# Pooling two batches of keys and one of values on GpSimd, the second layer of one more chunk by seven products, and another written-out order

## The chip, the cores and the metric

One NeuronCore of a Trainium2 chip runs the whole computation in one launch. It has five engines, each of which takes its instructions in the order in which they were written: TensorE (PE, with its weight loads as PEld), VectorE (DVE), ScalarE (ACT), GpSimd (POOL) and SyncE (SP, which here only issues transfers). The metric is the device time of one execution in microseconds (us); smaller is better.

## The reference

Attention over pooled keys and values, then a layer norm, a two-layer feed-forward net and a residual:

```
k_p = k.reshape(B, H, 72, 8, 64).mean(axis=3)      # B = H = 8, S = 576, D = 64
v_p = v.reshape(B, H, 72, 8, 64).mean(axis=3)
attn = softmax(q @ k_p^T / 8)                      # over the 72 pooled keys
x = (attn @ v_p), heads side by side               # 8 batches x 576 tokens x 512
xn = (x - mean) / sqrt(var + 1e-6) * g_ln
out = x + relu(xn @ w_ch1) @ w_ch2                 # 512 -> 2048 -> 512
```

All inputs and the output are float32.

## The kernel before

The 4608 tokens are cut into 36 tiles of 128 (t) and nine chunks of four tiles (c = 0 to 8). A tile goes through scores against the pooled keys (`scores`, L748), exponentials and their two float16 halves (`probs`, L776; for the first four tiles `probs_turned`, L803), attention times values, the token's mean and variance and the normalised z (`values`, L865), and z's split into two float16 halves. Every float16 product is made of three matmuls (high by high, high by low, low by high).

Keys and values are pooled once per batch b. `load_k`, `pool_k` (L620 to L630) take a pair of heads at a time: a transfer of 288 KB, one DVE reduction over 8 tokens (L627) and two DVE copies into the block-diagonal `kblk` (L630). `load_v`, `pool_v` (L632 to L640) take a head at a time: a transfer and one DVE reduction (L640). `max_v` and `split_v` (L642 to L720) scale the pooled values and split them, and `spread_v` (L725 to L729) copies them to other partitions by four small transfers, on SP's queue for b = 0 and 1 and on ACT's for later batches. The weights come as raw pairs of integers (`load_raw`, L484), are turned into float32 (`convert`, L489 to L530: DVE maximum L504, two ACT passes, DVE merge L520), get a common scale per half (`max_w1`, `max_w2`) and are split (`split_w` to `split`, L458 to L467).

Layer 1 of chunks 0 and 1 is plain (`ffn_in`, L1058 to L1081, matmul L1070). From chunk 2 on it is Strassen-Winograd's scheme, seven products in place of eight (`product`, L1105 to L1133, matmul L1114), on sums of z (L966 to L973) and of w1 (`sums_w`, L585 to L603). Layer 2 is plain for chunks 0 to 3: `ffn_out` (L1253 to L1276, matmul L1265) makes a tile's half of the sum with 24 matmuls of 512 columns, on the hidden layer that `whole_h` (L1135 to L1144) writes into the ring buffer. From chunk `C_TWO` = 4 on layer 2 is seven products too: `left_factors`, `right_relu`, `right_sums` and `right_pair` (L1154 to L1176, all through `split_h`, L1148 to L1152) make the factors of the hidden layer in the place of w2, and `out_seven` (L1224 to L1251, matmul L1231, sum L1248) makes a product's half with 12 matmuls of 256 columns. The factors of w2 for this are made once by `sums_w2` (L1186 to L1213, in 16 pieces) and `keep_w2`, are kept in DRAM and are brought back by `load_w2`, 512 KB each, 14 per chunk.

The order of all work is written out by hand in two lists of tokens, START (chunks 0 and 1, all preparation of weights, batches 0 to 3 of keys and values) and STEADY (the rest). A token names a step and its arguments; each time that it stands in the list, the step goes on to its next `yield` (`run`, L1360). So A.t is `scores` and `probs` of tile t, B.t `values`, E.t.i `probs_turned`, HK.b.i and HV.b.i half the heads of a batch's keys and values (turn by turn a transfer and its pooling), K0 and V0 batch 0's keys and values, LN, LK, Q, R transfers of tokens, keys, queries and raw weights, C `convert`, M1 and M2 the common scales, S `split_w`, F `ffn_in`, G `ffn_out`, T and U w1's sums, D `spread_v`, P `product`, WH `whole_h`, EL, ER, ES, EP the four factor steps, TW `sums_w2`, KW `keep_w2`, LW `load_w2`, O `out_seven`. Nothing is reordered behind these lists: each engine runs its instructions in list order and waits where an input or a buffer is not ready. START has three PSUM banks for the matmul groups of F and G, STEADY six.

Of the kernel before, what the change touches and what calls it, by code (L numbers as in the profile page):

```python
# [357 lines left out]
def attn_ffn_kernel(ctx: ExitStack, tc: tile.TileContext, qT, kT, v, kvn, kvt, g, w1, w2, out):  # L358
# [265 lines left out]
    def pool_k(b, p):  # L624
# [3 lines left out]
        for j in range(2):  # L628
            r, c = slice(j * D, (j + 1) * D), slice(j * KV, (j + 1) * KV)
            nc.vector.tensor_copy(out=kblk[b % NKB][r, p, c], in_=kp[r])  # L630
# [775 lines left out]
```

## Time and profile before

| | |
|---|---|
| median of 3 runs | 821.44 us (820.87 to 822.48) |
| the profiled execution | 825.36 us, span 823.6 us from the first to the last instruction |
| PE busy | 788.5 us, 96% of the span |
| DVE busy | 655.3 us, 80% |
| ACT busy | 453.5 us, 55% |
| POOL busy | 441.4 us, 54% |
| chain that ended last | PE 75%, DVE 16%, transfers 2%, ACT 2%, POOL 2% |
| mean granted TensorE clock | 0.990 |

A row of a group of instructions gives the line, the engine, the operation, what is written and read, shapes and count; behind the first bar the busy time and the mean duration of one (ns), behind the second the idle time of its engine just before, with what ended it. The view of stretches gives for each stretch of the span the busy time of each engine with its number of instructions, then the granted clock of TensorE, the busy share of the transfer engines and GB/s. Busy time is a union: instructions of one engine overlap at their ends, so means times counts come out somewhat higher.

### The profile page before, as it was taken

The page shows a single profiled execution, that of the slowest core. Times are in us where ns is not written, and L with a number is a line of the kernel's source. Part 1 is how long each engine was busy: PE and PEld are TensorE (multiplying, and loading weights), DVE is VectorE, ACT ScalarE, POOL GpSimd, SP SyncE. Part 2 cuts the span into 40 slices and gives each one's busy share as a digit, 9 for nine tenths or more (in the row PEclk, how much of TensorE's full clock was granted, in tenths as well). Part 3 has the DMA queues.
Part 4 walks back from the last instruction along what each step waited for, and adds up shares of the span by engine and source line. Part 5 has one row for each costly group of instructions (what it writes and reads, how often), then busy time and mean ns, then how long its engine had stood idle before and what let it go on. Part 6 is the DMA issues. An engine that isn't in the chain of part 4 may idle for free.

```text
span 823.6 us, 16934 instructions
## 1 busy us (share of the span) xinstructions
PE 788.5 (96%) x6462; PEld 595.7 (72%) x6462; DVE 655.3 (80%) x1328; ACT 453.5 (55%) x848; POOL 441.4 (54%) x521
## 2 busy tenths in 40 slices
...
GB/s 359 333 125 254 215 126 141 150 90 27 1 106 146 168 157 185 164 158 153 134 105 205 155 190 221 152 243 137 214 146 156 174 178 99 166 166 142 90 104 153
DMA packets 179201, 131.54 MB, mean 160 GB/s; under 512 B 143536, under 2 KB 150832, under 8 KB 176944
## 3 DMA queue, kind: packets, MB, share of 16 engines
...
q10 hardware_dynamic: 1152, 0.90, 0.5%
...
## 4 chain that ended last, share of the span: by engine, by line
PE 75%; DVE 16%; DMA 2%; ACT 2%; POOL 2%; issue 2%; ACTq 1%; DVEq 0%; POOLq 0%
PE ps_f L1114 29%; PE ps_f L1231 19%; PE ps_f L1265 13%; PE ps_f L1070 7%; PE ps_a L754 4%; DVE w L520 2%; DVE w L467 1%; PE ps_a L886 1%; DVE x L1248 1%; PE ps_m L694 1%; PE ps_a L887 1%; DMA vr<-in_v_dram 1%; DVE x L1276 1%; DVE raw L595 1%; DVE wm L504 1%
## 5 line engine op out<-in xcount | busy, mean ns | idle before, releaser
L1114 PE MATMUL ps_f<-zts,w 128*128 128x256 f16 x1680 | 207.2, 273 | 0.9 <-DVE x L1276 0.8
L1231 PE MATMUL ps_f<-ring,w 128*128 128x256 f16 x1680 | 193.7, 273 | 3.8 <-DVE x L1248 2.8
L1231 PEld LDWEIGHTS <-w 128*128 128x128 f16 x1680 | 163.7, 98 | 24.4 <-issue 4.0
L1114 PEld LDWEIGHTS <-w 128*128 128x128 f16 x1680 | 163.4, 98 | 22.1 <-issue 1.5
L1265 PE MATMUL ps_f<-w,ring 128*128 128x512 f16 x768 | 170.0, 379 | 1.5 <-DVE ring L1144 1.4
L1265 PEld LDWEIGHTS <-ring 128*128 128x128 f16 x768 | 74.2, 98 | 88.9 <-DVE ring L1144 3.6
L1133 ACT COPY raw<-ps_f 128x256 f32<-128x256 f32 x168 | 59.1, 372 | 94.3 <-PE ps_f L1114 87.5
L1152 POOL TENSOR_TENSOR w<-w 128x512 f16<-128x512 f32 x64 | 75.1, 1177 | 35.7 <-ACT w L1150 28.4
L1114 PE MATMUL ps_f<-zts,tsp 128*128 128x256 f16 x672 | 91.1, 273 | 0.8 <-ACT raw L1133 0.8
L1070 PE MATMUL ps_f<-zts,w 128*128 128x512 f16 (+1 forms) x480 | 88.4, 343 | 2.5 <-DVE x L1276 1.6
L790 POOL TENSOR_TENSOR phl<-e,phl 128x512 f16<-128x512 f32 x32 | 38.6, 1206 | 73.2 <-ACT phl L780 73.1
L1070 PEld LDWEIGHTS <-w 128*128 128x128 f16 x480 | 47.2, 99 | 40.4 <-issue 6.8
L1150 ACT CAST w<-w 128x512 f16<-128x512 f32 x80 | 48.9, 619 | 46.0 <-POOL w L1170 17.9
L1114 PEld LDWEIGHTS <-tsp 128*128 128x128 f16 x672 | 65.2, 98 | 9.4 <-issue 1.1
L1039 POOL TENSOR_TENSOR hl<-raw,hl 128x640 f16<-128x640 f32 x28 | 40.3, 1444 | 31.6 <-ACT hl L1037 23.2
L1248 DVE SCALAR_TENSOR_TENSOR x<-ps_f,y,x 128x256 f32<-128x256 f32 (+1 forms) x70 | 35.4, 518 | 26.2 <-PE ps_f L1231 25.6
L1248 DVE SCALAR_TENSOR_TENSOR x<-ps_f,cy,x 128x256 f32<-128x256 f32 (+1 forms) x70 | 35.2, 516 | 17.3 <-PE ps_f L1231 16.8
L1128 DVE TENSOR_TENSOR raw<-ps_f,raw 128x256 f32<-128x256 f32 x84 | 34.0, 416 | 18.5 <-PE ps_f L1114 9.6
L754 PE MATMUL ps_a<-kblk,q 128*128 128x144 f32 (+1 forms) x320 | 41.9, 289 | 1.7 <-issue 1.2
L754 PEld LDWEIGHTS ps_a<-kblk,q 128*128 128x128 f32 (+1 forms) x320 | 37.0, 179 | 4.9 <-issue 2.4
L1039 POOL TENSOR_TENSOR hl<-z,hl 128x512 f16<-128x512 f32 x18 | 23.9, 1327 | 30.8 <-ACT hl L1037 16.5
L1079 ACT ACTIVATE ring<-ps_f 128x512 f16<-128x512 f32 (+1 forms) x40 | 19.5, 508 | 37.9 <-PE ps_f L1070 33.3
...
## 6 DMA issues: line engine op xcount, KB each, us to landing
...
```

The lines of the kernel that those rows point to most:

```text
L754: nc.tensor.matmul(ps[r, p // 2, p % 2 * 2 * KV : (p % 2 + 1) * 2 * KV], lhsT=q[:, p, r], rhs=kblk[b % NKB][:, p, :], start=True, stop=True,)
L790: nc.gpsimd.tensor_tensor(out=ph[:, 0, :, KA:P], in0=e[:, :, 0:KA], in1=ph[:, 0, :, 0:KA], op=ALU.subtract)
L1039: nc.gpsimd.tensor_tensor(out=zhl[:, 1, :], in0=src, in1=zhl[:, 0, :], op=ALU.subtract)
L1070: nc.tensor.matmul(ps, lhsT=w[:, part, fs], rhs=zT[:, kz, cols], start=(n == 0), stop=(n == 3 * NKT - 1),)
L1114: nc.tensor.matmul(ps, lhsT=w[:, part, f * P : (f + 1) * P], rhs=z, start=m in (1, 2, 4, 5) and n == 0, stop=m in (2, 3, 4, 7) and n == 3 ...
L1128: nc.vector.tensor_tensor(out=o, in0=ps, in1=o, op=ALU.add)
L1133: nc.scalar.copy(out=o, in_=ps)
L1150: nc.scalar.copy(out=hi, in_=src)
L1152: engine.tensor_tensor(out=lo, in0=src, in1=hi, op=ALU.subtract)
L1231: nc.tensor.matmul(ps, lhsT=wt[2][:, left, part, f * HC + u * P : f * HC + (u + 1) * P], rhs=b[:, f // FPB, wp, f % FPB], start=n < 4 and ...
L1248: nc.vector.scalar_tensor_tensor(out=x, in0=ps, scalar=scale, in1=x, op0=ALU.mult, op1=ALU.add)
L1265: nc.tensor.matmul(ps, lhsT=h[:, part, i, cols], rhs=w[:, wp, j], start=(n == 0), stop=(n == 3 * NFT // 2 - 1),)
```

## The change

Four things change.

1. `pool_k` runs on GpSimd for batches 1 and 2, and `pool_v` for batch 1: three additions of halves (8 to 4, 4 to 2, 2 to 1) take the place of one reduction; for keys the last addition writes `kblk`, once for each of the two heads, so the copies go. The host lays these batches out with the 8 tokens outermost; the bytes of the transfers are the same.
2. `C_TWO` goes from 4 to 3: chunk 3's second layer becomes `out_seven`, with factor steps in place of `whole_h`, and 14 reloads of w2's factors.
3. `LO_GPSIMD` goes from (6, 7, 8) to (): the low halves of `right_pair` with i = 0 in chunks 6, 7 and 8 go from GpSimd to VectorE (24 instructions).
4. Both lists are written anew. In STEADY all 16 TW and 6 KW steps now stand in chunk 2 and at the start of chunk 3. In START, of what the prediction speaks of: the order of the first transfers, A.0 ahead of V0, the places of pooling steps, and B.9 behind HV.2.1.

In `values` the place where a scratch tile is named moves, with the same instructions.

```diff
-C_TWO = 4
+C_TWO = 3
-LO_GPSIMD = (6,7,8)
+K_GPSIMD, V_GPSIMD = (1, 2), (1,)
+LO_GPSIMD = ()
 START = """
-LN.2 LN.2 LK.0 LK.0 LK.1 LK.1 Q.0 Q.0 HK.1.0 R.1.0 R.1.0 V0 V0 K0 K0 K0 HK.1.0 HK.1.0 Q.1 Q.1 R.1.1 R.1.1 R.1.2 R.1.2
-A.0 R.1.3 R.1.3 LG LG A.0 A.0 A.0 E.0.0 V0 V0 E.0.1 A.1 HV.1.0 R.2.0 R.2.0 HK.1.1 A.1 C.1.0 C.1.0 V0 V0 E.0.0 HK.1.0
...
-S.1.2 E.3.1 B.2 E.3.0 E.3.0 S.1.2 S.1.2 S.1.3 C.2.2 C.2.1 E.3.1 E.3.1 B.3 HK.1.1 HK.1.1 R.2.3 R.2.3 A.4 R.1.4 R.1.4 B.1
-B.1 HK.1.1 HK.1.1 A.4 A.5 S.1.3 S.1.3 F.0.0.0 F.0.1.0 F.0.0.0 B.2 F.0.1.0 A.4 A.5 F.0.2.0 A.4 F.0.2.0 C.2.2 HV.1.0
...
-A.8 F.0.7.1 M1.1 B.4 A.6 A.6 A.9 S.2.1 S.2.1 S.2.2 C.1.4 F.0.6.1 S.2.2 S.2.2 S.2.3 F.0.7.1 A.7 C.1.5 C.1.6 F.0.5.1
...
-G.0.1.1 G.0.1.1 HK.3.0 HV.2.1 A.10 HV.2.1 HV.2.1 G.0.3.1 A.11 HV.2.1 HV.2.1 B.8 T.1.0 HV.2.1 HV.2.1 HV.2.1 HV.2.1 A.11
-B.9 F.1.0 F.1.0 T.1.0 HV.3.0 HV.3.0 A.10 A.10 G.0.2.1 A.11 B.9 V.10 F.1.1 F.1.1 HV.3.0 HV.3.0 G.0.2.1 G.0.2.1 A.11 A.11
...
+LK.0 LK.0 Q.0 Q.0 LK.1 LK.1 LN.2 LN.2 R.1.0 R.1.0 HK.1.0 Q.1 Q.1 R.1.1 R.1.1 K0 K0 K0 C.1.0 C.1.0 HK.1.0 HK.1.0 R.1.2
+R.1.2 A.0 R.1.3 R.1.3 A.0 V0 V0 A.0 A.0 E.0.0 E.0.1 E.0.0 E.0.1 A.1 LG LG HV.1.0 HK.1.1 R.2.0 R.2.0 A.1 V0 V0 C.1.1
...
+B.3 B.0 B.0 B.1 A.4 S.1.2 S.1.2 S.1.3 A.4 C.2.2 C.2.1 B.1 B.1 S.1.3 S.1.3 HV.1.0 HV.1.0 B.3 HV.1.1 HV.1.1 B.2 A.4
+HV.1.1 HK.2.0 HK.2.0 D.0 D.0 HV.1.1 A.5 A.4 A.4 A.5 B.2 F.0.0.0 F.0.1.0 F.0.2.0 F.0.0.0 F.0.1.0 C.2.3 F.0.2.0 F.0.0.0
...
+B.4 M1.1 F.0.6.1 C.1.5 F.0.7.1 A.6 A.6 B.4 B.5 C.1.4 C.1.4 C.1.6 C.1.6 S.2.3 S.2.3 G.0.0.0 B.5 B.6 M1.1 M1.1 S.1.4
...
+A.11 F.0.15 B.7 F.0.15 S.2.6 S.2.6 S.2.7 A.10 HV.3.0 HV.3.0 A.10 A.10 B.7 F.0.14 F.0.14 HV.2.1 HV.2.1 HV.2.1 S.2.7
+S.2.7 F.0.15 F.0.15 G.0.0.1 G.0.1.1 G.0.2.1 HV.3.0 HV.3.0 B.6 B.6 HV.3.1 G.0.0.1 G.0.0.1 G.0.0.1 A.11 T.1.0 T.1.0
+HV.3.0 HV.3.0 G.0.1.1 T.1.0 T.1.0 B.8 B.9 G.0.3.1 HV.3.1 HV.3.1 G.0.1.1 G.0.1.1 HV.3.1 G.0.2.1 B.9 V.10 HK.3.0 HK.3.0
...
     def pool_k(b, p):
         kr = kraw.pop((b, p))
-        kp = kr.rearrange("p k l -> p (k l)")[:, 0:KV]
-        nc.vector.tensor_reduce(out=kp, in_=kr, axis=AX.X, op=ALU.add)
+        if b in K_GPSIMD:
+            kr = kr.rearrange("p k l -> p (k l)").rearrange("p (l k) -> p l k", k=KV)
+            nc.gpsimd.tensor_add(out=kr[:, 0:4, :], in0=kr[:, 0:4, :], in1=kr[:, 4:8, :])
+            nc.gpsimd.tensor_add(out=kr[:, 0:2, :], in0=kr[:, 0:2, :], in1=kr[:, 2:4, :])
+        else:
+            kp = kr.rearrange("p k l -> p (k l)")[:, 0:KV]
+            nc.vector.tensor_reduce(out=kp, in_=kr, axis=AX.X, op=ALU.add)
         for j in range(2):
             r, c = slice(j * D, (j + 1) * D), slice(j * KV, (j + 1) * KV)
-            nc.vector.tensor_copy(out=kblk[b % NKB][r, p, c], in_=kp[r])
+            if b in K_GPSIMD:
+                nc.gpsimd.tensor_add(out=kblk[b % NKB][r, p, c], in0=kr[r, 0, :], in1=kr[r, 1, :])
+            else:
+                nc.vector.tensor_copy(out=kblk[b % NKB][r, p, c], in_=kp[r])
...
         vr = vraw.pop((b, h))
-        nc.vector.tensor_reduce(out=vp[b][:, h, :], in_=vr, axis=AX.X, op=ALU.add)
+        if b not in V_GPSIMD:
+            nc.vector.tensor_reduce(out=vp[b][:, h, :], in_=vr, axis=AX.X, op=ALU.add)
+            return
+        vr = vr.rearrange("p d l -> p (d l)").rearrange("p (l d) -> p l d", d=D)
+        nc.gpsimd.tensor_add(out=vr[:, 0:4, :], in0=vr[:, 0:4, :], in1=vr[:, 4:8, :])
+        nc.gpsimd.tensor_add(out=vr[:, 0:2, :], in0=vr[:, 0:2, :], in1=vr[:, 2:4, :])
+        nc.gpsimd.tensor_add(out=vp[b][:, h, :], in0=vr[:, 0, :], in1=vr[:, 1, :])
```

601 lines of the change are left out of this document (311 added, 290 removed).

## The prediction, written before the result was known

> **What bounds the kernel now.** I read the stretches of the span first, then TensorE's waits, then the chain of waits, then VectorE's timeline. Stretches (us: length; busy time and instructions of PE, PEld, DVE, ACT, POOL; granted clock, transfers):
>
> ```profile
> 0.00:50.30 50.30, 38.27 (x314) 29.18 (x314) 40.77 (x76) 32.66 (x42) 17.29 (x25) 0.93 0.81 304
> 50.30:85.00 34.70, 29.51 (x272) 25.02 (x270) 30.83 (x68) 30.41 (x50) 14.13 (x15) 1.00 0.74 195
> 85.00:150.00 65.00, 64.96 (x367) 32.19 (x366) 62.31 (x123) 42.71 (x57) 27.67 (x25) 1.00 0.65 172
> 150.00:165.00 15.00, 12.42 (x71) 5.77 (x70) 9.23 (x20) 2.52 (x4) 3.33 (x5) 0.77 0.63 121
> ...
> 245.00:340.00 95.00, 92.78 (x760) 66.85 (x759) 78.36 (x179) 48.20 (x97) 40.01 (x59) 1.00 0.64 155
> 340.00:440.00 100.00, 98.75 (x737) 67.47 (x736) 83.65 (x177) 50.10 (x104) 52.14 (x73) 1.00 0.65 157
> ...
> 600.00:824.00 224.00, 215.78 (x2046) 192.23 (x2044) 149.94 (x298) 125.41 (x259) 153.75 (x173) 0.99 0.50 140
> ```
> From 245 us, where START's last matmul ends, PE is busy nearly all the time: 2.2 us are free in 245 to 340, 1.3 in 340 to 440. There only fewer matmuls can help. START is different. Up to 50.3 us PE lacks 12.0 us, up to 85 another 5.2, and in 150 to 165 another 2.6 at a granted clock of 0.77 (a loss of (1 - 0.77) x 15 = 3.5 us). DVE is busy 30.8 of 34.7 us before 85 and 62.3 of 65 after it. So START is set by what VectorE must do before PE can go on.
>
> ```profile
> PE ps_m L694 <- DMA w<-in_kvn_dram: 6.2, 1, 6.2
> ...
> PE ps_a L886 <- DMA va<-vh: 2.6, 1, 2.6
> ```
> ```profile
> 6.21 7.32 PE ps_m L694 x10
> ...
> 50.40 2.73 PE ps_f L1070 x24
> ...
> 150.90 4.50 DMA va<-vh
> ...
> 224.33 20.73 PE ps_f L1265 x96
> ...
> 799.63 18.36 PE ps_f L1231 x168
> ```
> The waits name the first and the late hole: the first matmul waits 6.2 us for tokens, and attention times values waits 2.6 us for `va`, the spread values of batch 2, a transfer of 4.50 us. VectorE's timeline shows the middle:
>
> ```profile
> 8.10 1.35 DVE L1336 TENSOR_REDUCE w<-w 128x144 f32<-128x1152 f32 x1 [5.31 <-DMA w<-in_kT_dram]
> ...
> 15.53 0.68 DVE L644 TENSOR_REDUCE mv<-vp 72x1 f32<-72x512 f32 x1
> ...
> 49.90 1.28 DVE L467 SCALAR_TENSOR_TENSOR w<-w,gs 128x1024 f16<-128x1024 f32 x1
> ```
> At 8.10 us batch 0's keys are there, at 15.53 V0's maximum begins, and at 49.90 + 1.28 = 51.2 us the last split of w1's first half ends, which the first layer-1 matmuls (50.40) need. Between 15.53 and 51.2 DVE is idle for hardly a moment.
>
> **The change, part by part.** The sum is made against the profiled execution (825.36 us, span 823.6), which is 3.9 us above the median of 821.44; I take the differences and subtract them from the median.
>
> *Chunk 3's second layer.* Plain: 2 halves x 4 tiles x 24 = 192 matmuls at 20.73 / 96 = 216 ns, 41.5 us. Seven products: 2 x 7 x 2 x 12 = 336 at 18.36 / 168 = 109 ns, 36.7 us. On the path, since PE is full there: -4.7 us. What comes with it:
>
> ```profile
> L1248 DVE SCALAR_TENSOR_TENSOR x<-ps_f,y,x 128x256 f32<-128x256 f32 x60 | 28.2, 480 | 21.1 <-PE ps_f L1231 20.7
> ...
> L1144 DVE SCALAR_TENSOR_TENSOR ring<-raw,ring 128x512 f16<-128x512 f32 x32 | 23.6, 781 | 2.1 <-ACT ring L1140 2.0
> ...
> L1169 POOL TENSOR_TENSOR w<-raw 128x256 f32<-128x256 f32 x26 | 21.2, 814 | 34.0 <-ACT raw L1161 32.6 <-DVE w L1152 0.9
> ...
> L1276 DVE SCALAR_TENSOR_TENSOR x<-ps_f,cy,x 128x512 f32<-128x512 f32 x28 | 20.7, 742 | 2.6 <-PE ps_f L1265 2.1
> ...
> L1152 DVE TENSOR_TENSOR w<-raw,w 128x512 f16<-128x512 f32 x26 | 19.2, 746 | 2.5 <-ACT w L1150 2.5
> L1206 POOL TENSOR_TENSOR phl<-kr,phl 128x512 f16<-128x512 f32 x16 | 18.8, 1180 | 12.4 <-ACT phl L1204 7.9 <-DMA w2s<-phl 4.6
> ...
> L1152 DVE TENSOR_TENSOR w<-raw,w 128x256 f16<-128x256 f32 x26 | 15.3, 588 | 2.4 <-ACT w L1150 2.4
> L1193 DVE TENSOR_TENSOR kr<-w 128x256 f32<-128x256 f16 x32 | 13.9, 475 | 2.1 <-POOL phl L1206 2.0
> ...
> L1152 DVE TENSOR_TENSOR w<-w 128x512 f16<-128x512 f32 x16 | 13.7, 858 | 0.3 <-ACT w L1150 0.3
> ...
> L1199 POOL TENSOR_TENSOR kr<-kr 128x128 f32<-128x128 f32 x16 | 7.6, 478 | 1.3
> ```
> DVE loses 8 x 0.742 (sums) and 16 x 0.781 (`whole_h`) = 18.4 us and gets 24 sums of 0.480, 4 double ones at about 0.742, and 8 x (0.746 + 0.588 + 0.858) of splits = 32.0 us: +13.6. The eight DVE pairs of w2's second half (16 x 0.475 = 7.6) go from chunk 3 to chunk 2. So DVE comes to 78.4 + 7.6 = 86 of 95 us in chunk 2 and 83.7 - 7.6 + 13.6 = 90 of about 95 in chunk 3: hidden, with little room. POOL's piece of `sums_w2` is four additions near 0.478 and one of 1.18, 3.1 us; eight of them, 24.7 us, move to chunk 2 (40.0 becomes 65 of 95), and chunk 3 gets 8 x (4 x 0.814 + 1.18) = 35.5 (52.1 becomes 63). ACT is half idle in 340 to 440. 14 reloads of 512 KB are 7.3 MB in 95 us, some 77 GB/s on 157, below the 304 that the first stretch carries. Queued behind the new POOL and DVE steps are PSUM sums (L1248, L1128) and with them PE's banks. I take +2 us of new waits for all this, between 0 and 5 (half of DVE's 10 us of room gone).
>
> *`LO_GPSIMD`.* 24 subtractions leave POOL (24 x 1.18) and cost DVE 24 x 0.858 = 20.6 us in 600 to 824, where it is busy for 149.9 of 224 us: nothing; without that room, 20.6.
>
> *Pooling.* Rows of what goes, of narrow GpSimd additions, and of two DVE steps that are moved:
>
> ```profile
> L640 DVE TENSOR_REDUCE vp<-vr 72x64 f32<-72x512 f32 x56 | 37.1, 673 | 3.2 <-DMA vr<-in_v_dram 3.1
> ...
> L764 DVE TENSOR_REDUCE mx<-ps_a 128x8 f32<-128x576 f32 x36 | 27.0, 751 | 13.5 <-PE ps_a L754 13.2
> ...
> L769 DVE TENSOR_TENSOR e<-ps_a,mx 128x576 f32<-128x576 f32 x32 | 24.2, 758 | 2.4
> ...
> L630 DVE COPY kblk<-kr 64x72 f32<-64x72 f32 x56 | 20.9, 373 | 1.3
> L627 DVE TENSOR_REDUCE kr<-kr 128x72 f32<-128x576 f32 x28 | 20.8, 742 | 0.1
> ...
> L793 POOL TENSOR_TENSOR phl<-e,phl 128x64 f16<-128x64 f32 x32 | 13.7, 428 | 0.0
> ```
> Off DVE: 8 pairs x (0.742 + 2 x 0.373) + 8 heads x 0.673 = 17.3 us. Onto POOL: the trace has no such addition, but its neighbours. Keys: 288 wide between 0.814 (256) and 1.18 (512), nearest 0.88; 144 wide 0.52 (0.478 at 128); two of 72 at 0.43 each: 2.3 us a pair. Values: 0.81 + 0.48 + 0.43 = 1.7 us a head. In all 32 us, in a queue that was busy for 31.4 of the first 85 us. Batch 1 alone makes 23 of it and comes before 85: 54. Ahead of the first tiles' low halves of z (L858), which the first layer-1 matmuls need, stand batch 1's four pairs and three heads, 14 us more than the at most 17 so far: from the first landing, which I estimate near 12.5 us by the rate below, that ends by 44 plus waits, below 50. So hidden, but not by much.
>
> *START's order, up to the first layer-1 matmul.* The keys (two transfers of 576 KB) and Q.0 (256 KB) now go ahead of the tokens (1152 KB). Before, tokens had landed at 6.21 and the first 576 KB of keys at 8.10: 303 KB/us after 2.4 us of start. So all keys are there at about 7, K0 ends at 8.9, and V0's matmuls, 7.3 us, run from 10.9 to 18.2 instead of 6.2 to 13.5. V0's maximum moves from 15.5 to about 18.8, and DVE, in order, waits for it. From there to the last split it had 35.7 us. It sheds three pairs (3 x 1.49), one head (0.67) and one maximum of w1 (1.21, done while it waits), and gets A.4's scores (0.751 + 0.758) and a merge (1.22): -3.6. The last split ends at 18.8 + 32.1 = 50.9: no gain (between -2 and +2), but A.4 is done.
>
> *From there to layer 2 of chunk 0 (85.0).*
>
> ```profile
> 73.34 0.68 DVE L640 TENSOR_REDUCE vp<-vr 72x64 f32<-72x512 f32 x1 [2.50 <-DMA vr<-in_v_dram]
> ...
> 83.52 0.15 DVE L425 TENSOR_SCALAR rowmax<-rowmax 128x1 int32<-128x1 int32 x1
> ...
> 84.99 5.35 PE L1265 MATMUL ps_f<-w,ring 128*128 128x512 f16 x24
> ```
> DVE reached the end of M1.1's row maxima at 83.7 us, 32.5 after the split. A.4 and the merge are done (-2.7), seven heads are gone (-4.7), the wait of 2.50 for values' transfers falls on POOL, and two small steps come ahead (at most a merge's 1.2): 23.8, so about 75. Then PE is the bound: it was busy for 29.5 of the 34.7 us, has one score step less and one small step more (29.0, an estimate half a us lower): so 79.4. ACT, 30.4 busy less A.4's three steps, has nearly as much to do: +1. Layer 2 (L1265) at 80.4 instead of 85.0: -4.6 us, between 0 (nothing) and -6.
>
> *The spread of batch 2.* Before, its transfer is issued directly ahead of B.9 in PE's order; now G.0.0.1, G.0.1.1 and G.0.2.1 (3 x 24 x 216 ns = 15.5 us) lie between. That covers 4.50 us. The hole of 2.6 us and the low clock behind it (3.5) go: up to -6.1; at worst 0, if VectorE comes to the split later. I take -5.
>
> *Two engines on one port.* The pooled batches went through DVE's reductions; the additions read two operands.
>
> ```profile
> L520 DVE SCALAR_TENSOR_TENSOR w<-w,tsp x8: 1211/1217/1231, 21.9 to 116.3; 128x1024 int32<-128x1024 int32 x8
> ...
> L520 DVE SCALAR_TENSOR_TENSOR w<-w,ring x2: 1216/1698/2180, 37.5 to 38.7; 128x1024 int32<-128x1024 int32 x2
> ...
> L858 POOL TENSOR_TENSOR zts<-z,zts x4: 1152/1160/2226, 37.5 to 63.0; 128x512 f16<-128x512 f32 x4
> ```
> DVE's merge takes 1.22 us, once 2.18; POOL's subtraction 1.15, once 2.23, at the same moment (37.5): both lose 1 us. POOL gets 23 us more in the first 85 us, from 37% busy to 64%; of DVE's some 16 wide merges and splits there about 4 more are hit, and the POOL ones with them. I take +2.5, from 0 to 6. The Trainium skill (SBUF — State Buffer, section "Who interferes with whom") says that a DVE instruction with two SBUF inputs contends for a whole instruction with a GpSimd one that reads SBUF, and a reduction never does. That speaks against this move; the two long rows agree, and by it alone every one of the 16 could be hit, a sum 13 us worse.
>
> Sum: -4.7 + 2 - 4.6 - 5 + 2.5 = -9.8 us: **811.6** (span near 814).
>
> **Rivals.**
> 1. *Only the products count.* The late V0 takes what the lighter DVE gives, PE reaches layer 2 at 85 as before, and another spread waits instead (D.1 stands 4 us ahead of B.4). For it: ACT is as full as DVE before 85. Against: DVE's list is shorter by 17.3 us. 821.4 - 4.7 + 1 = 817.7.
> 2. *START gains all and nothing is lost.* -6 - 6.1 - 4.7: 804.6. For it: PE was full for 65 us beside a DVE busy for 62.3 of them. Against: the port rows.
> 3. *The products bring nothing:* chunk 3's factors and reloads come late by the 4.7 us, START stays: 821.4. For it: these factors pass through DVE and POOL before PE has them, and both get fuller in this stretch. Against: with DVE at 83.7 of 100 PE lost 1.3 us.
> 4. *Slower: GpSimd late in front of chunk 3.* All 16 pieces of w2's sums must be in DRAM and read out before chunk 3's first factor may overwrite w2. 16 x 3.1 + the other 15.3 us of that stretch = 65 us of POOL in PE's 95. This decides once port conflicts stretch POOL by more than 95 / 65 = 1.47; the worst row stretches by 2226 / 1152 = 1.93, the median not at all. At 1.6 it is 104, 9 late, and 3.5 at low clock: 811.6 + 12.5 = 824.1. The Trainium skill (TensorE: Matmul & The Clock Gate, Part 1) has the clock at half until about 3.4 us of work have gone by, a loss of half of that; in 150 to 165 the loss is twice as large, 3.5 us, and the row decides.
>
> **How the numbers follow.** Forecast 0.36, rival 1 0.26, rival 2 0.15, rival 3 0.10, rival 4 0.13. A median of this kernel is known to some 0.2% (1.6 us; its three runs spread by that). Faster: forecast, rivals 1 and 2, a little of 3: 0.78. Same: most of 3, 0.08. Slower: rival 4 and a part of the open waits, 0.14. The bounds of the forecast's terms reach from rival 2's 804.6 to 827; leaving out 2 in 10, 804 to 823.5.
>
> **What would show it.** Right: L1231 x2016 and L1265 x576; PE's matmuls of the first layer near 50 us and of layer 2 near 80; no wait for `va` with a clock under 1 near 150; PE free for about 2 us per 100 in chunks 2 and 3; L627 x20, L640 x48, and 56 new POOL additions. Wrong: V0's maximum later than 20 us or the first layer-1 matmul after 53; merges (L520) often near 2 us; PE waiting in chunk 3 for factors, sums or `ring`; VectorE full and PSUM sums late in chunks 2 to 5.

## The result and the profile after

The changed kernel takes 831.25 us (median of 4 runs, 830.86 to 831.60) beside 821.15 us for the kernel before on the same chip. The ratio is 1.0118, with a 95% interval of 1.0102 to 1.0135: slower by 1.2%, where 1.2% faster had been forecast. The profiled execution has a span of 829.9 us (before: 823.6). Its stretches, in the columns explained above:

```profile
0.00:50.30 50.30, 38.57 (x312) 29.61 (x312) 35.90 (x64) 30.22 (x39) 29.78 (x47) 0.97 0.77 286
50.30:85.00 34.70, 29.42 (x271) 25.35 (x271) 30.92 (x59) 33.53 (x52) 29.77 (x42) 1.00 0.77 242
85.00:150.00 65.00, 62.15 (x340) 30.53 (x341) 62.59 (x112) 42.56 (x57) 34.29 (x32) 0.95 0.72 175
150.00:165.00 15.00, 15.00 (x110) 7.54 (x108) 14.33 (x32) 4.27 (x8) 6.46 (x9) 1.00 0.84 206
...
243.00:300.00 57.00, 55.23 (x462) 40.71 (x462) 49.13 (x109) 28.75 (x60) 31.85 (x49) 1.00 0.75 185
300.00:340.00 40.00, 33.74 (x230) 21.41 (x229) 35.94 (x75) 18.98 (x37) 29.62 (x41) 0.96 0.55 126
...
480.00:520.00 40.00, 32.66 (x286) 27.78 (x286) 31.79 (x60) 18.78 (x36) 17.66 (x24) 0.96 0.52 139
```

The same two late stretches of the kernel before:

```profile
300.00:340.00 40.00, 38.63 (x284) 25.49 (x283) 33.49 (x79) 21.64 (x43) 21.68 (x31) 1.00 0.64 156
...
480.00:520.00 40.00, 39.64 (x382) 35.62 (x380) 32.12 (x67) 22.92 (x45) 21.09 (x25) 1.00 0.94 225
```

Two things are to be seen. Up to 85 us GpSimd is busy for 59.6 us in place of 31.4, and PE is no better off. And PE, which lacked 1.4 and 0.4 us in the two late stretches, now lacks 6.3 in 300 to 340 and 7.3 in 480 to 520, each at a granted clock of 0.96. TensorE's waits (us in total, times, longest) name who is late; some 29 of the 38 us are put down to VectorE:

```profile
PE ps_a L785 <- DVE kblk L1370: 7.3, 2, 6.6
PE ps_f L1262 <- DVE w L1183: 4.6, 5, 3.3
PE ps_a L917 <- DVE x L935: 3.8, 1, 3.8
PE ps_f L1262 <- DVE x L1279: 3.8, 3, 2.2
PE ps_f L1145 <- DVE raw L1159: 3.0, 2, 2.1
...
PE ps_f L1296 <- DVE x L1307: 2.8, 1, 2.8
```

(Lines have moved: L754 is now L785, L1070 L1101, L1114 L1145, L1152 L1183, L1231 L1262, L1248 L1279, L1265 L1296, L1276 L1307.) The wait for `va` of before is gone. The first row is no new loss: 6.6 us of it are the first matmul's wait for batch 0's keys, in the place of the 6.2 us for tokens of before.

What VectorE did around the hole at 490 to 501 (three waits of PE, 6.3 us together) stands in its timeline (start, length, line, operation):

```profile
492.06 1.11 DVE L1032 TENSOR_TENSOR a<-y 128x4 f32<-128x4 f32 x1
493.20 0.23 DVE L1033 TENSOR_TENSOR a<-a,ve 128x4 f32<-128x4 f32 x1
493.47 1.32 DVE L1034 SCALAR_TENSOR_TENSOR y<-a,y 128x4 f32<-128x4 f32 x1
494.71 0.47 DVE L1279 SCALAR_TENSOR_TENSOR x<-ps_f,y,x 128x256 f32<-128x256 f32 x1
495.10 0.79 DVE L1032 TENSOR_TENSOR a<-y 128x4 f32<-128x4 f32 x1
495.93 1.32 DVE L1033 TENSOR_TENSOR a<-a,ve 128x4 f32<-128x4 f32 x1
497.29 0.65 DVE L1034 SCALAR_TENSOR_TENSOR y<-a,y 128x4 f32<-128x4 f32 x1
...
499.45 1.05 DVE L1034 SCALAR_TENSOR_TENSOR y<-a,y 128x4 f32<-128x4 f32 x1
```

The split of L1183 that PE waits for (3.3 us) comes right behind, at 500.42. These are the refinement steps of chunk 5's token scales (`token_scales`): nine operations on 128 x 4 numbers, seven of them shown. In the views of their lines the median length is 0.16 us; here the nine come to 6.8. GpSimd's timeline beside them:

```profile
491.81 1.34 POOL L821 TENSOR_TENSOR phl<-e,phl 128x512 f16<-128x512 f32 x1
...
493.38 1.39 POOL L1070 TENSOR_TENSOR hl<-raw,hl 128x640 f16<-128x640 f32 x1
494.73 1.15 POOL L1183 TENSOR_TENSOR w<-w 128x512 f16<-128x512 f32 x1
495.84 1.40 POOL L1070 TENSOR_TENSOR hl<-raw,hl 128x640 f16<-128x640 f32 x1
497.20 0.72 POOL L1203 TENSOR_TENSOR w<-raw,w 128x256 f32<-128x256 f32 x1
...
499.33 1.15 POOL L1183 TENSOR_TENSOR w<-w 128x512 f16<-128x512 f32 x1 [0.73 <-ACT w L1181]
```

Each long small operation ends within 0.04 us of the end of a GpSimd instruction: 493.17 and 493.15, 494.79 and 494.77, 495.89 and 495.88, 497.25 and 497.24, 497.94 and 497.92, 500.50 and 500.48. The sum of L1279 in the middle, which reads PSUM, takes its ordinary 0.47. So a first theory: a small VectorE operation waits for a whole GpSimd instruction, and whatever stands behind it in VectorE's queue, and PE, waits too.

In START the same picture stands ahead of PE's wait of 3.8 us (VectorE, then PE, then GpSimd):

```profile
82.33 2.77 DVE L924 COPY cvm<-cv 64x3 f32<-64x3 f32 x2
...
85.70 0.69 DVE L935 TENSOR_TENSOR x<-ps_a,rs 128x512 f32<-128x512 f32 x1
```
```profile
86.54 0.21 PE L917 MATMUL ps_a<-va,pt 128*128 128x65 f16 x1 [3.84 <-DVE x L935]
...
87.39 3.17 PE L1296 MATMUL ps_f<-w,ring 128*128 128x512 f16 x7
```
```profile
82.19 2.13 POOL L481 TENSOR_TENSOR w<-w 128x1024 f16<-128x1024 f32 x1 [2.63 <-ACT w L479]
```

Two copies of 64 x 3 numbers take 2.77 us beside a GpSimd subtraction of 2.13.

### The profile page after: what moved, and what is told of

Read it like the earlier page. It is cut to its first block, busy times and chain, and to the rows that moved or that the text cites. A ratio compares the mean times of both kernels' runs of the same rounds, so it can differ in the third digit from the quotient of the medians.

```text
span 829.9 us, 17329 instructions
## 1 busy us (share of the span) xinstructions
PE 787.7 (95%) x6606; PEld 612.1 (74%) x6606; DVE 661.5 (80%) x1348; ACT 468.8 (56%) x880; POOL 482.5 (58%) x593
## 4 chain that ended last, share of the span: by engine, by line
PE 74%; DVE 18%; POOL 4%; ACT 2%; issue 1%; DMA 1%; SPq 0%; DVEq 0%; POOLq 0%
PE ps_f L1145 26%; PE ps_f L1262 23%; PE ps_f L1296 11%; PE ps_f L1101 7%; PE ps_a L785 3%; DVE w L1183 2%; DVE w L537 2%; DVE x L1279 1%; PE ps_a L917 1%; PE ps_a L918 1%; DVE mx L795 1%; PE ps_m L725 1%; DVE w L484 1%; DVE x L1307 1%; DVE kr L1224 1%
## 5 line engine op out<-in xcount | busy, mean ns | idle before, releaser
L1262 PE MATMUL ps_f<-ring,w 128*128 128x256 f16 x2016 | 235.2, 274 | 8.9 <-DVE w L1183 4.6
L1262 PEld LDWEIGHTS <-w 128*128 128x128 f16 x2016 | 196.9, 98 | 35.9 <-DVE w L1183 6.3
L1145 PE MATMUL ps_f<-zts,w 128*128 128x256 f16 x1680 | 207.8, 273 | 1.0 <-DVE x L1307 0.8
L1145 PEld LDWEIGHTS <-w 128*128 128x128 f16 x1680 | 163.4, 98 | 21.6 <-issue 1.8
L1296 PE MATMUL ps_f<-w,ring 128*128 128x512 f16 x576 | 128.9, 384 | 2.9 <-DVE x L1307 2.8
L1296 PEld LDWEIGHTS <-ring 128*128 128x128 f16 x576 | 56.6, 99 | 70.7 <-issue 6.3
L1145 PE MATMUL ps_f<-zts,tsp 128*128 128x256 f16 x672 | 92.7, 276 | 6.2 <-DVE raw L1159 3.0
L1101 PE MATMUL ps_f<-zts,w 128*128 128x512 f16 (+1 forms) x480 | 85.7, 336 | 2.9 <-POOL zts L889 1.5
L1181 ACT CAST w<-w 128x512 f16<-128x512 f32 x96 | 58.7, 619 | 51.8 <-POOL w L1204 27.1
L1145 PEld LDWEIGHTS <-tsp 128*128 128x128 f16 x672 | 66.0, 99 | 15.9 <-issue 7.3
L1183 POOL TENSOR_TENSOR w<-w 128x512 f16<-128x512 f32 x48 | 58.0, 1208 | 32.9 <-ACT w L1181 21.2
L1101 PEld LDWEIGHTS <-w 128*128 128x128 f16 x480 | 46.5, 98 | 38.4 <-issue 4.2
L1279 DVE SCALAR_TENSOR_TENSOR x<-ps_f,y,x 128x256 f32<-128x256 f32 (+1 forms) x84 | 42.7, 517 | 33.5 <-PE ps_f L1262 32.9
L1200 POOL TENSOR_TENSOR w<-raw 128x256 f32<-128x256 f32 x32 | 25.7, 802 | 62.4 <-ACT raw L1192 33.0
L1279 DVE SCALAR_TENSOR_TENSOR x<-ps_f,cy,x 128x256 f32<-128x256 f32 (+1 forms) x84 | 42.1, 516 | 15.4 <-PE ps_f L1262 14.8
L785 PE MATMUL ps_a<-kblk,q 128*128 128x144 f32 (+1 forms) x320 | 43.7, 294 | 9.5 <-DVE kblk L1370 7.3
L1070 POOL TENSOR_TENSOR hl<-raw,hl 128x640 f16<-128x640 f32 x28 | 40.6, 1453 | 13.1 <-ACT hl L1068 13.1
L785 PEld LDWEIGHTS ps_a<-kblk,q 128*128 128x128 f32 (+1 forms) x320 | 38.2, 183 | 12.4 <-DVE kblk L1370 7.7
L1183 DVE TENSOR_TENSOR w<-raw,w 128x512 f16<-128x512 f32 (+1 forms) x64 | 42.6, 667 | 2.5 <-ACT w L1181 2.4
L1159 DVE TENSOR_TENSOR raw<-ps_f,raw 128x256 f32<-128x256 f32 x80 | 32.2, 417 | 13.9 <-PE ps_f L1145 8.0
```

What stands on the lines that cost most here:

```text
L785: nc.tensor.matmul(ps[r, p // 2, p % 2 * 2 * KV : (p % 2 + 1) * 2 * KV], lhsT=q[:, p, r], rhs=kblk[b % NKB][:, p, :], start=True, stop=True,)
L1070: nc.gpsimd.tensor_tensor(out=zhl[:, 1, :], in0=src, in1=zhl[:, 0, :], op=ALU.subtract)
L1101: nc.tensor.matmul(ps, lhsT=w[:, part, fs], rhs=zT[:, kz, cols], start=(n == 0), stop=(n == 3 * NKT - 1),)
L1145: nc.tensor.matmul(ps, lhsT=w[:, part, f * P : (f + 1) * P], rhs=z, start=m in (1, 2, 4, 5) and n == 0, stop=m in (2, 3, 4, 7) and n == 3 ...
L1159: nc.vector.tensor_tensor(out=o, in0=ps, in1=o, op=ALU.add)
L1181: nc.scalar.copy(out=hi, in_=src)
```

## The experiments

All ratios are to the kernel before, run beside each kernel, with 95% intervals. Its own median was 822.6 to 823.3 us in these series, so differences between kernels are taken between their ratios, times 822.5 us, and not between their times. The rival theory throughout is that VectorE simply has too much to do in these places, in any order and whatever GpSimd does.

### Where the loss lies: START, STEADY, pooling

*e1*: the changed kernel with the old STEADY list.

```diff
-C_TWO = 3
+C_TWO = 4
-LO_GPSIMD = ()
+LO_GPSIMD = (6, 7, 8)
-STEADY = (new list)
+STEADY = (list of the kernel before)
```

> The changed kernel with the old STEADY list (chunk 3's second layer plain, low halves of chunks 6 to 8 on GpSimd): of the change, only START's order and the pooling on GpSimd are left. Theory (START is worth the 2 us by which its last matmul came earlier, 243.0 instead of 245.1, and the loss is all in STEADY): 819 us, 817 to 821. Rival A (START hands over something late, a key, a value or a sum, that STEADY pays for): 824 or more. Rival B (START's gain was real but eaten behind it by the new STEADY only): 814 or less.

Measured: 822.8 us, ratio 1.0006 (0.9992 to 1.0021). START's order and the pooling together are worth nothing; the theory's 2 us, read off one matmul, were not there.

*e2*: the other half, with the old START and the pooling on VectorE.

```diff
-K_GPSIMD, V_GPSIMD = (1, 2), (1,)
+K_GPSIMD, V_GPSIMD = (), ()
-START = (new list)
+START = (list of the kernel before)
```

> The old START list with the old pooling on VectorE, and the new STEADY list (chunk 3 by seven products, all low halves of right_pair on VectorE). Theory (the loss is STEADY's): the 2 us of START come back on top of 831.3, so 833 us, 830 to 836, with the holes near 305, 330 and 490 us still there, 2 us later. Rival A (the loss comes from START or from pooling on GpSimd): 817, the old time less the 4.7 us of the products.

Measured: 831.3 us, 1.0102 (1.0069 to 1.0135). All of the loss is STEADY's, and it doesn't need the pooling or the new START.

*e3*: both new lists, pooling back on VectorE (the first two lines of e2's diff).

> The changed kernel with both lists as they are, and all pooling back on VectorE (K_GPSIMD and V_GPSIMD empty). If GpSimd is the engine that the front of START waits for (theory: it stands in the chain of waits from 30 to 65 us), the first layer-1 matmul comes earlier than 53.1 us, but VectorE, 93 of 100 us busy from 50 to 150, gets 17 us more and layer 2 of chunk 0 comes later than 87.4: 834 us, 831 to 838. Rival (what the pooling on GpSimd costs in conflicts is as much as it saves): 829 to 831, START's last matmul within 1 us of 243.

Measured: 839.6 us, 1.0202 (1.0174 to 1.0230), 6.9 us slower than the change. The direction was expected, one part of the reason was not: the first layer-1 matmul comes at 59.7 us, not before 53.1, and layer 2 of chunk 0 at 98.2. With this order VectorE can't carry the pooling.

### The hole at 490 us

*e4*: the nine operations with one input each.

```diff
-nc.vector.tensor_tensor(out=a, in0=y, in1=y, op=ALU.mult)
-nc.vector.tensor_tensor(out=a, in0=a, in1=ve, op=ALU.mult)
-nc.vector.scalar_tensor_tensor(out=y, in0=a, scalar=1.5, in1=y, op0=ALU.subtract, op1=ALU.mult)
+nc.vector.tensor_scalar(out=a, in0=y, scalar1=1.0, scalar2=0.0, op0=ALU.mult, op1=ALU.add)
+nc.vector.tensor_scalar(out=a, in0=a, scalar1=1.0, scalar2=0.0, op0=ALU.mult, op1=ALU.add)
+nc.vector.tensor_scalar(out=y, in0=a, scalar1=-1.0, scalar2=0.0, op0=ALU.mult, op1=ALU.add)
```

> The changed kernel, with each of the three operations of the three refinement steps of the token scales (128 x 4 elements, on VectorE) replaced by one that reads one tensor in place of two: the same number, size, place and engine. Left out is the refinement itself, so the scales are rough. Theory (at 492 to 500 us these nine each wait for a whole GpSimd instruction because both read two tensors; 1.46 us of work takes 6.9, and the splits behind them on VectorE, and so TensorE's factors, come late by that): the nine fall back to 0.16 us each, the hole of 6.3 us there goes with the low clock behind it, and the time is 824 us, 822 to 826. Rival (VectorE simply has too much to do there and the order is wrong): 831, 830 to 832, with the hole in its place.

Measured: 833.3 us, 1.0122 (1.0091 to 1.0153): no gain. Taken alone this speaks for the rival. VectorE's timeline says otherwise:

```profile
493.55 1.12 DVE L1032 TENSOR_SCALAR a<-y 128x4 f32<-128x4 f32 x1
494.70 0.23 DVE L1033 TENSOR_SCALAR a<-a 128x4 f32<-128x4 f32 x1
494.96 1.32 DVE L1034 TENSOR_SCALAR y<-a 128x4 f32<-128x4 f32 x1
```

The one-input operations last as long as the two-input ones, to 0.01 us; the three shown here end within 0.03 us of a GpSimd instruction. The experiment had not removed the wait, so it could not tell the theories apart; what fell is "because both read two tensors". The Trainium skill (SBUF — State Buffer, section "Who interferes with whom") has this: beside operations with two inputs in SBUF it lists copies and TENSOR_SCALAR as able to contend with GpSimd, in the modes in which they use two ports for one tensor, and says of reductions that they never do on this chip. The rows of e4 agree with the first half (no row shows the mode), those of e5 with the second.

*e5*: the same nine as reductions over an axis of length 1.

```diff
-(the three operations)
+nc.vector.tensor_reduce(out=a, in_=y.unsqueeze(2), axis=AX.X, op=ALU.add)
+nc.vector.tensor_reduce(out=a, in_=y.unsqueeze(2), axis=AX.X, op=ALU.add)
+nc.vector.tensor_reduce(out=y, in_=a.unsqueeze(2), axis=AX.X, op=ALU.add)
```

> As e4_one_input, but each of the nine operations is a reduction over an axis of length 1 (TENSOR_REDUCE, 128 x 4 out of 128 x 4 x 1). In e4 the one-input TENSOR_SCALAR had waited just as long as the two-input ones (1.12, 0.23, 1.32 us for 1.11, 0.23, 1.32), so it didn't tell contention from order. The rows of the changed kernel beside GpSimd's work show reductions at their ordinary time (0.67 us for values at 501.0). Left out are the refinement and the sign of the scales. Theory (these nine wait for GpSimd's instructions, and the rest of VectorE's queue and TensorE behind it): about 0.16 us each at 492 to 500, the hole of 6.3 us gone, 824 us, 822 to 826. Rival (VectorE's list is too long there whatever the operations): 831, 830 to 833.

Measured: 824.8 us, 1.0024 (1.0010 to 1.0038), 7.7 us less than the change, as the theory had it (7.3). (The reduction at 501.0 us that the expectation points to had no GpSimd instruction beside it, so it showed nothing yet.) Same place, number and size; only the form differs:

```profile
492.44 0.14 DVE L1032 TENSOR_REDUCE a<-y 128x4 f32<-128x4 f32 x1
492.62 0.16 DVE L1033 TENSOR_REDUCE a<-y 128x4 f32<-128x4 f32 x1
492.81 0.16 DVE L1034 TENSOR_REDUCE y<-a 128x4 f32<-128x4 f32 x1
492.88 0.47 DVE L1277 SCALAR_TENSOR_TENSOR x<-ps_f,y,x 128x256 f32<-128x256 f32 x1
```

0.16 us each where they had been up to 1.32. From 480 to 520 us PE is busy for 36.5 us in place of 32.7, at a clock of 1.00 in place of 0.96, which is some 5.5 us of the 7.7; the rest lies elsewhere, since the steps of all chunks were changed. This settles the cause of most of that hole: not the amount of VectorE's work, and not the order by itself, but small operations that wait for GpSimd, in front of work that PE needs.

*e6*: the order instead of the form.

```diff
-... TS.5 O.4.1.1.1 O.4.1.1.1 TS.5 HV.6.1 ... A.24 TS.5 EP.4.1.3.0 ... HK.6.0 HK.6.0 O.4.1.6.0 ...
+... O.4.1.1.1 O.4.1.1.1 HV.6.1 ... A.24 EP.4.1.3.0 ... HK.6.0 HK.6.0 TS.5 TS.5 TS.5 O.4.1.6.0 ...
```

> The changed kernel with one edit of order: the three refinement steps of chunk 5's token scales (tokens TS.5, nine operations of 128 x 4), whose result is first needed near 550 us, stand some 50 tokens later, behind HK.6.0, where GpSimd has a pause. Same work, same forms. Theory (they stood in front of the splits and sums that TensorE waits for while GpSimd ran six instructions in a row): the hole at 490 to 501 shrinks from 6.3 us to 1 or less and takes the low clock behind it with it (1.8 us): 824 us, 822 to 826. Rival (VectorE is full there and the next operation is late instead): 829 or more.

Measured: 827.2 us, 1.0043 (1.0028 to 1.0059), 6.2 us less than the change: near the theory's 7.3, far from the rival. All nine take 0.16 to 0.17 us there. Between 480 and 507 us PE still loses 3.8 us in six waits of 0.2 to 0.9 us; four of them had been there, two (one for GpSimd, one for VectorE) are new.

*e7*: the refinement on GpSimd, with four operations a step.

```diff
-nc.vector.tensor_tensor(...), nc.vector.tensor_tensor(...), nc.vector.scalar_tensor_tensor(...)
+nc.gpsimd.tensor_tensor(out=a, in0=y, in1=y, op=ALU.mult)
+nc.gpsimd.tensor_tensor(out=a, in0=a, in1=ve, op=ALU.mult)
+nc.gpsimd.tensor_scalar(out=a, in0=a, scalar1=1.5, scalar2=1.0, op0=ALU.subtract, op1=ALU.mult)
+nc.gpsimd.tensor_tensor(out=y, in0=a, in1=y, op=ALU.mult)
```

> The changed kernel with the refinement of all token scales on GpSimd in place of VectorE (four operations a step, as the fused one isn't used there; some 0.15 to 0.25 us each). Theory: at 492 to 500 VectorE is free of the wait, 824 us, 822 to 827; GpSimd's queue gets 12 small operations a chunk, 2 to 3 us, with room. Rival (GpSimd is what is late at this place, its sums feed the splits): 831 or more.

Measured: 828.1 us, 1.0059 (1.0040 to 1.0079), 4.9 us less than the change: the theory holds, with less to gain than by moving.

*e8*: e6, and chunk 3's token scales later too.

```diff
-... TS.3 TW.1.2.0 TS.3 TS.3 TS.3 G.2.0.1 ... P.3.0.2.6 P.3.0.2.6 ...
+... TW.1.2.0 G.2.0.1 ... P.3.0.2.6 TS.3 TS.3 TS.3 TS.3 P.3.0.2.6 ...
```

> As e6_ts5_later, and the last steps of chunk 3's token scales (TS.3, at 326 to 330 us in front of a sum for which TensorE waits 2.8 us) stand 130 tokens later too; their result is first needed near 360. Theory: 2.2 us of stretched small operations leave that place, the wait of 2.8 falls to 1 or less: 821.5 us, 819.5 to 824. Rival: as e6, 824, because the sum there is late for other reasons.

Measured: 825.0 us, 1.0026 (1.0015 to 1.0037). PE's wait of 2.8 us for L1307 is gone; a new one of 1.6 us ends at 357 (at 352 in e12, where START is shorter), ahead of which the moved operations now lie (nine; the expectation of e14 counts them as eleven). Against e6 it is 1.4 us less (expected 2.5). Moving 7 tokens of 3398 has brought 7.6 us of STEADY's loss back.

### START

*e9*: the change with one line edited.

```diff
-nc.vector.tensor_copy(out=cv[r], in_=CV[b][r])
+nc.vector.tensor_reduce(out=cv[r], in_=CV[b][r].unsqueeze(2), axis=AX.X, op=ALU.add)
```

> The changed kernel with the two copies of 64 x 3 elements that tiles over a batch's border need (line 924, eight instructions in the whole span) written as reductions over an axis of length 1: the same values. In START they took 2.77 us at 82.3 us beside a GpSimd instruction of 2.13, ordinarily 0.3, and TensorE waited 3.84 us there for what follows them. Theory (START's expected gain goes into such waits behind GpSimd): that hole shrinks by 2.4 us, layer 2 of chunk 0 begins near 85 instead of 87.4, and since TensorE is full from there to 243 all of it and some of the clock's loss stays: 828.5 us, 827 to 829.5. Rival (the splits of w1 and the sums of values in the same queue are late anyway): 831.

Measured: 828.0 us, 1.0061 (1.0040 to 1.0082), 4.7 us less than the change, somewhat more than expected (2.8). VectorE and PE at that place:

```profile
82.27 0.30 DVE L924 TENSOR_REDUCE cvm<-cv 64x3 f32<-64x3 f32 x2
```
```profile
84.01 0.19 PE L917 MATMUL ps_a<-va,pt 128*128 128x65 f16 x1 [1.38 <-DVE x L935]
```

2.77 us became 0.30, PE's wait of 3.84 became 1.38, and layer 2 of chunk 0 begins at 84.5 in place of 87.4.

*e10* is e8 with e9's line, *e11* is e1 with e9's line, *e17* is the kernel before with it.

> e8_ts3_ts5_later and the copies of e9_cvm_reduce together. Theory: the two add, 825.0 less 2.4 to 3.5: 822 us, 820.5 to 823.5. Rival (what comes earlier in START is lost again in STEADY, where VectorE is full): 824.5 or more.

> The new START with pooling on GpSimd, the old STEADY (chunk 3 plain), and the copies of line 924 as reductions. Theory: 822.8 less 2.4 to 3.5, so 820 us, 818.5 to 821, less than the kernel before. Rival: 822.8, as without the edit.

> The kernel before with one edit: the copies of line 893 (64 x 3, tiles over a batch's border) as reductions. Of the eight, one took 1.5 us there and none stands in front of a wait of TensorE. Theory (the 4 us of e11 are START's new order, freed of its worst wait): no change, 823, 822 to 824. Rival (the edit is worth as much in any kernel): 820 or less.

Measured: e10 821.2 us, 0.9976 (0.9961 to 0.9991), 4.1 less than e8; e11 **818.8 us, 0.9952 (0.9937 to 0.9968)**, 4.4 less than e1 and faster than both kernels; e17 823.0 us, 0.9989 (0.9969 to 1.0009), no change. All three go the theory's way: the line is worth its wait where it stands ahead of PE, and nothing elsewhere.

*e13*: e11 with two of the three additions of each pooling left out.

```diff
-nc.gpsimd.tensor_add(out=kr[:, 0:4, :], in0=kr[:, 0:4, :], in1=kr[:, 4:8, :])
-nc.gpsimd.tensor_add(out=kr[:, 0:2, :], in0=kr[:, 0:2, :], in1=kr[:, 2:4, :])
-nc.gpsimd.tensor_add(out=vr[:, 0:4, :], in0=vr[:, 0:4, :], in1=vr[:, 4:8, :])
-nc.gpsimd.tensor_add(out=vr[:, 0:2, :], in0=vr[:, 0:2, :], in1=vr[:, 2:4, :])
```

> e11_e1_cvm (new START, old STEADY, copies as reductions; 818.8 us) with only the last of the three halvings of each pooled key pair and value head on GpSimd: left out are the first two, so 6 of 8 tokens, and 8 x 1.29 + 8 x 1.2 = 20 us of GpSimd's work up to 107 us. Theory (what START was expected to gain and did not is taken by GpSimd's additions and the waits of VectorE behind them): first layer-1 matmul near 51 in place of 53, START's end 2 to 4 us earlier: 815.5 us, 814 to 817. Rival (the order has no more to give; the first transfers and VectorE's own list set it): 818 to 819.

Measured: 814.3 us, 0.9891 (0.9867 to 0.9916), 5.0 us less than e11. The first layer-1 and layer-2 matmuls of e13, then those of e11:

```profile
50.58 0.60 PE L1081 MATMUL ps_f<-zts,w 128*128 128x256 f16 x4
...
80.36 0.81 PE L1276 MATMUL ps_f<-w,ring 128*128 128x512 f16 x3
```
```profile
53.31 0.93 PE L1085 MATMUL ps_f<-zts,w 128*128 128x256 f16 x7
...
84.81 1.04 PE L1280 MATMUL ps_f<-w,ring 128*128 128x512 f16 x3
```

The forecast had 50.9 and 80.4. With most of GpSimd's additions gone both places are reached when they were forecast, and the additions are what the order is short of: 2.7 us at layer 1, 4.5 at layer 2, 5.2 at START's end (235.5 in place of 240.7). How much of that is GpSimd's own queue and how much VectorE's waits behind it, this run can't tell: it takes both away. In the chain of waits of the changed kernel GpSimd is the path from 51.2 to 71.7 us, and the pooling's additions are 11.1 us of that.

### What is left in STEADY

*e12* is e10 with batch 4's keys on GpSimd too, *e14* is e12 with TS.3's steps at a third place, *e16* is e14 with the keys of batches 5 to 7 on GpSimd as well.

```diff
 e12: -K_GPSIMD = (1, 2)      +K_GPSIMD = (1, 2, 4)
 e14: -... P.3.0.2.6 TS.3 TS.3 TS.3 TS.3 ...   +... P.3.0.3.3 P.3.0.3.3 TS.3 TS.3 TS.3 TS.3 EL.3.0.3 ...
 e16: -K_GPSIMD = (1, 2, 4)   +K_GPSIMD = (1, 2, 4, 5, 6, 7)
```

> e10_e8_cvm with the keys of batch 4 pooled on GpSimd too: four reductions and eight copies (4 x 1.12 us) leave VectorE at 282 to 299 us, where they stand in front of the sums and hidden halves for which TensorE waits 4.2 us at 302 to 307, and GpSimd, which waits 5.96 and 5.99 us for VectorE there, gets 4 x 2.1. Theory A (in chunk 2 VectorE has too much to do, not only waits behind GpSimd): 2 to 4 us less than e10. Theory B (what counts there is the waits behind GpSimd, and these get more): no change or 1 to 3 us more.

> e12_keys4_gp (820.2 us) with TS.3's last steps at a third place, behind P.3.0.3.3 near 357 us, where both VectorE and GpSimd pause. At the second place (344 to 347 us) eleven small operations take 2.7 us in front of a score step, and TensorE waits 1.62 us at 352. Theory: that wait goes, nothing new comes: 818.5 us, 817.5 to 819.5. Rival (VectorE is full there in any order): 820 or more.

> e14_ts3_third (819.5 us) with the keys of batches 5, 6 and 7 on GpSimd too: 12 reductions and 24 copies, 13.4 us, leave VectorE between 360 and 600 us, GpSimd gets 12 x 2.1 = 25 us there. Theory A (VectorE has too much to do in chunks 3 to 5): as for batch 4, 0.3 us a pair, 816 to 818. Theory B (what is left are waits of VectorE behind GpSimd): 819.5 to 822.

Measured: e12 820.2 us, 0.9959 (0.9945 to 0.9972); e14 819.5 us, 0.9957 (0.9937 to 0.9976); e16 823.0 us, 0.9998 (0.9981 to 1.0015). The steps from e10 to e12 and from e12 to e14 are each within what the intervals leave open (e12 was between its two theories); the wait of 1.6 us at 352 is gone in e14, its small operations take 0.15 to 0.23. e16 is 3.4 us slower than e14, as the theory of waits has it: VectorE's busy time falls by 7.1 us, where the expectation had 13.4 us of work leave it, and PE waits more often.

*e15* is e12 and *e18* is e11, each with the other setting of `LO_GPSIMD`.

```diff
 e15: -LO_GPSIMD = ()          +LO_GPSIMD = (6, 7, 8)
 e18: -LO_GPSIMD = (6, 7, 8)   +LO_GPSIMD = ()
```

> e12_keys4_gp with the low halves of right_pair of chunks 6 to 8 back on GpSimd, as before the change (24 subtractions). Forecast on record for this part: nothing, hidden in VectorE's room from 600 us on: 820, 819 to 821.5. Rival (fewer wide instructions on GpSimd are fewer waits for VectorE, and the change gained by it): 822 or more. Rival (VectorE was nearer to its limit there): 818.5 or less.

> e11_e1_cvm (818.8 us: new START, pooling on GpSimd, old STEADY, copies of line 924 as reductions) with the low halves of right_pair of chunks 6 to 8 on VectorE, as in the change. Theory (24 wide subtractions fewer on GpSimd are fewer waits of VectorE, worth the 1.2 us that e15 lost): 817.6 us, 816.5 to 818.5. Rival (hidden in VectorE's room, as forecast): 818.8.

Measured: e15 821.4 us, 0.9982 (0.9967 to 0.9996), 1.9 more than e12, with intervals that overlap; e18 822.1 us, 0.9987 (0.9969 to 1.0005), 2.9 more than e11, with intervals that just don't. So the 24 subtractions on VectorE do no harm with the new list and cost 2.9 us with the old one; why, no run shows. The expectation for e18, which carried e15's number to another list, was wrong.

## Why the prediction was wrong

START's end is the first product of chunk 2, and STEADY is the span less that (us, one profiled execution each):

| | first layer 1 | first layer 2 | START's end | STEADY |
|---|---|---|---|---|
| before | 50.3 | 85.0 | 245.9 | 577.7 |
| forecast | 50.9 | 80.4 | 238.8 | 575.0 |
| changed kernel | 53.1 | 87.4 | 243.8 | 586.1 |
| e11 (old STEADY) | 53.3 | 84.8 | 240.7 | 576.1 |
| e13 (old STEADY, few additions) | 50.6 | 80.4 | 235.5 | 577.0 |
| e14 (new STEADY, mended) | 53.4 | 85.0 | 240.8 | 576.9 |

(The forecast's two ends are its terms: 245.9 - 4.6 - 5 + 2.5 and 577.7 - 4.7 + 2.)

1. **"I take +2 us of new waits for all this, between 0 and 5" is the step that failed most.** STEADY came out 11 us above the forecast. The amounts of work were right: VectorE 85.1 of 97 us from 243 to 340 (forecast 86 of 95), GpSimd 61.5 (forecast 65). What failed is the inference from "room left" to "hidden". Small operations of the token scales of chunks 3 and 5 stood where GpSimd's instructions came one behind the other; the forecast counted neither. Moving seven tokens gave 7.6 back (e8), changing the operations' form 7.7 (e5, all chunks). Another 1.6 went with e12 and e14 together, not each beyond doubt. What remains are short waits near 302 and 475 to 500 us, and no run tried them by themselves. The longest of them, 2.1 us for L1159 (L1158 in e14), looks in the trace like a wide case of the same kind. In the changed kernel, two rows of VectorE and one of GpSimd:

```profile
301.95 2.82 DVE L1175 SCALAR_TENSOR_TENSOR ring<-raw,ring 128x512 f16<-128x512 f32 x2
...
305.35 1.28 DVE L1175 SCALAR_TENSOR_TENSOR ring<-raw,ring 128x512 f16<-128x512 f32 x2
```
```profile
302.37 1.85 POOL L1070 TENSOR_TENSOR hl<-raw,hl 128x640 f16<-128x640 f32 x1
```

Two splits of the hidden layer take 2.82 us beside a GpSimd subtraction of 1.85 (ordinarily 1.40), the next two 1.28.

2. **Pooling: "So hidden, but not by much" failed.** The cost came out right: in the groups of the changed kernel keys take 2.5 us a pair and values 1.7 a head (forecast 2.3 and 1.7), 34 us in all for the 32 forecast. That is partly luck: by the median lengths it would be 2.0 and 1.5, and stretched instructions make up the rest. And the additions are not hidden: e13 shows 5.0 us of the time behind two of the three additions. e3 shows the other side, 6.9 us more with the pooling on VectorE. So the part is worth having, and not free.

3. **Two engines on one port: "+2.5, from 0 to 6" left out the small operations.** I looked for the cost in wide merges and splits, each losing 1 us. There VectorE's loss was of the size forecast: the eight merges (L537) ahead of 85 us take 13.0 us where eight times 1.21 are 9.7; before, one merge had lost 1 us. What of this TensorE lost, no run shows. But the smallest operations, which the term put at nothing, cost more, since PE waits right behind: 4.1 to 4.7 us for one pair of 64 x 3 copies (e9 to e11).

4. **START's order: the times were right, with some luck.** Without most of GpSimd's additions, and with line 924's copies as reductions, the first layer 1 is at 50.6 and layer 2 at 80.4 us, as forecast. The steps to them were off both ways: in e13 V0's maximum begins at 16.2 us (forecast 18.8; 17.0 in the changed kernel), and from there to the last split VectorE takes 34.3 us (forecast 32.1). Behind it VectorE reaches the end of M1.1's row maxima at 78.0, not 75; PE, busy for 28.1 of the 29.8 us between the two places, is the bound as the forecast had it.

5. **The spread of batch 2: right.** The wait for `va` is gone, 150 to 165 us has a full PE at a clock of 1.00. No run gives its worth alone; in the changed kernel START ends only 2.1 us earlier than before, with the hole at 82 to 86 us and a clock of 0.95 in 85 to 150 ahead of it.

6. **The products: "-4.7" was too large.** The groups of e11 (plain chunk 3) and of e10 (seven products), both without a large hole in chunk 3:

```profile
L1246 PE MATMUL ps_f<-ring,w 128*128 128x256 f16 x1680 | 193.6, 273 | 2.6 <-DVE x L1263 2.2 <-DVE w L1167 0.2
L1280 PE MATMUL ps_f<-w,ring 128*128 128x512 f16 x768 | 171.6, 382 | 1.4 <-DVE ring L1159 1.4
```
```profile
L1261 PE MATMUL ps_f<-ring,w 128*128 128x256 f16 x2016 | 233.5, 273 | 4.3 <-DVE x L1278 1.5 <-DVE w L1182 1.3 <-POOL w L1182 0.8
L1295 PE MATMUL ps_f<-w,ring 128*128 128x512 f16 x576 | 128.1, 381 | 0.3 <-DVE ring L1174 0.2
```

336 more of the one take 39.9 us, 192 fewer of the other 43.5: 3.6 us, of which 0.4 is a difference in START, where both kernels have the same matmuls. The seven products were mis-sized most, 119 ns each for 109: the row they were priced by is the kernel's last, unbroken stretch. No run shows the gain in its time: STEADY is 576.9 us in e14 with the products and 576.1 in e11 without.

7. **`LO_GPSIMD`: "nothing" holds for this list only** (e15), not for the old one (e18).

**The rivals.** Rival 4 had the sign, not the mechanism: GpSimd was not late in front of chunk 3, its last piece of w2's sums began at 346.5 us and the first factor's split at 350.1, TensorE has no wait between 338 and 362 us, and the holes lie elsewhere. "VectorE full and PSUM sums late in chunks 2 to 5", named as what would make the forecast wrong, is what the profile shows at first sight; by e5 and e6 it was waits, and not work, that filled VectorE in the largest hole. The sentence on the Trainium skill (SBUF — State Buffer, section "Who interferes with whom") in the prediction was used for the wide operations alone, where the rule there speaks of whole instructions without regard to size. The small ones in front of PE were to be looked for too, and the profile of before had one: a copy of 64 x 3 (L893) of 1.52 us.
